# Joint products completed in place in two buffers, two more h blocks stored without their sums, premade sums at a wider pace

## The chip, the cores and the metric

One core of a Trainium2 chip runs the whole kernel in one launch. The metric is the device time of one execution in microseconds. All matrix products run on TensorE (PE in the profile), elementwise work on VectorE (DVE) and ScalarE (ACT); transfers are issued from the queues of SyncE (SP), GpSimd (POOL) and, for the very last store, ScalarE. The profile's times are microseconds from the span's start.

## The reference, cut to what matters

```python
a = einsum("bsd,ed->bse", x, dft_hid_re);  b = einsum("bsd,ed->bse", x, dft_hid_im)
A = einsum("ts,bse->bte", dft_seq_re, a) - einsum("ts,bse->bte", dft_seq_im, b)   # Fourier mixing
gate = einsum("bsd,df->bsf", x, W_gate);   up = einsum("bsd,df->bsf", x, W_up)
B = einsum("bsf,fd->bsd", where(gate > 0, gate, 0) * up, W_down)                  # gated MLP
g = sigmoid((x * gate_w).sum(-1))
return g * A + (1 - g) * B          # S = 2048, D = 512, F = 1792, float32
```

## The kernel before, in words

Every matrix operand is float32. It is split into a high part (a cast on ScalarE) and a low part (a subtraction on VectorE), and each product is three matmuls of 128x128 by 128x512: high by low, low by high, high by high. In the trace the parts carry h and l at the end of their names: xh and xl are the input's, wah, wal, wb0h, wb1l and wd the gate and up weights', lh and ll the down weights', ch and cl the right operands' of the later stages, wh and wl the left operands' of the last stage.

Products are done by schemes of the Strassen kind: seven products of sums of blocks (numbered 1 to 7) in place of eight, and for the sequence transform 26 products, one to a turn. The kernel's stages in order are:

1. **Gate and up**, blocks c = 0 to 6 of F for each half q of the sequence (q is 0 or 1). Blocks 0 and 1 of the first half come first, then c = 2 to 6 with both halves. A block ends with h, the product of the rectified gate and of up. From c = 3 on, class `Joined` computes one of the seven products (product 2 of gate and up) for both halves together by a second scheme over halves and blocks, class `JointW`, with seven short steps of three matmuls; from c = 4 on (`FOURS`) product 4 is treated the same way. I call these the joint steps 1 to 7. Their results leave PSUM by ScalarE copies or VectorE adds and are added to the block's own sums in `done` and `last`. Joint weights are made from the block's weights (buffers jws, jw); jx and kx are the joint right operands, jv and jo the joint intermediate values and results, u the sums of gate and up before the last multiplication.
2. **The hidden transform** (`SpectralBlock`), with blocks 0 and 1 of the second half of gate and up between.
3. **Two down rounds** (`Down`, one for each half of the sequence), whose right operands hr are read back from HBM (tensor hd).
4. **The sequence transform** (`Sequence`), 26 turns of 48 matmuls each, whose operands r and l are read from HBM and summed on the way; results are kept in PSUM or in js buffers and combined at the turns' ends.

h goes to HBM in `h_out`. Normally `h_sums` makes two pairs of sums of it on VectorE (buffers hs, four additions of 512 columns) and stores seven forms in all, which the down round reads. A pair of blocks named in the set `RAW`, as (half, pair), is stored without sums, as four forms; then the down round reads four and makes four sums itself (`made`).

Sums of the sequence matrices that many turns share are made early. `form_stored` makes them by DMA alone: a copy into HBM (tensor td) and then an accumulating transfer onto it, both from POOL's queue, paced by a small token instruction each. `form_rights` and `form_lefts` make others on VectorE (buffers rt, lt): two loads, one sum, one store. `put` is a store from SP's queue, `store` one from POOL's. In `form_stored(values, first, gap)` each of the four parts of a value takes two gaps, counted in matmuls.

The order of the work is not written out. Every step has a key, the number of the matmul beside which it is wanted, and a planner (`Plan`) simulates the engines. VectorE's and ScalarE's steps are sorted by a due time worked out backwards from the matmuls that need them; a step may run up to 40 matmuls ahead of its key. Steps that no matmul waits for get a due time from their key (`REST`), capped near the end of the program. Buffers (a "unit" each) are taken from 51 in all, the one idle longest first, so an instruction that first writes a buffer waits for the last user of its former tenant, a store among them. `LEAD`, `RAMP` and `FORM_LEAD` say how many matmuls ahead of use the sequence stage's operands are loaded, summed and split; `prepared` says the same for gate and up weights.

The lines of the joint step and of its results that the change touches most:

```python
slots = {(5, 1): (5, 1), (6, 1): (6,), (7, 0): (3, 7), (3, 0): (2, 4)}   # after which product which joint steps run
two, one = buf("jv"), buf("jv6", (N,))
self.s = {1: two[:, 0], 5: two[:, 1], 6: one[:]}
self.o = [buf(f"jo{q}") for q in range(2)]
```

Of the kernel before, what the change touches and what calls it, by code (L numbers as in the profile page):

```python
# [15 lines left out]
N = 512  # L16
# [2 lines left out]
NT, KD, KF = S // N, D // P, F // P  # L19
HD = D // 2  # L20
UNITS = 51
FOURS, FOUR_KEY, FOUR_W = 4, -100, 40

# [38 lines left out]
DIRECT, PLACE = (9, 10, 11, 14, 15, 20, 21), (0, 2, 3, 1)  # L64
GROUP = {9: 1, 10: 0, 11: 1, 14: 1, 15: 0, 20: 0, 21: 0}
ROOM = {'r': 6, 'l': 4}
LEAD = {'r': {'load': 56, 'sum': 56, 'sums': 8, 'draws': 30, 'hi': 42, 'lo': 34}, 'l': {'load': 40, 'sum': 46, 'sums': 8, 'draws': 56, 'hi': 55, 'lo': 48}}
RAMP = 50
FORM_LEAD = 43


def walk(side, blocks, room, ready=(), drawn={}):
# [197 lines left out]
class Plan:  # L270
# [47 lines left out]
    def due(self):  # L318

        last, n = {}, self.now  # L320
        for s in reversed(self.steps):
            if s.engine == "tensor" and s.key >= 0:
                n -= s.writes[0].size() / N
            if s.engine == "tensor":
                last[s] = min(last.get(s, 1e9), n * self.MATMUL)
            elif s not in last or s.key > 0:
                last[s] = min(last.get(s, 1e9), min(s.key + self.REST, self.now - 8) * self.MATMUL)
            s.due = last[s] - (s.work + self.LANDING if s.name == "dma_start" else 0)
            for x in s.after:
                last[x] = min(last.get(x, 1e9), s.due - self.WAIT - (x.work if x.name != "dma_start" else 0))  # L330
# [91 lines left out]
def kernel(ctx: ExitStack, tc, xP, xG, wgu, wd, cr, ci, wri, gw, out):  # L422
# [66 lines left out]
    def E():  # L489
        return plan  # L490
# [118 lines left out]
    FORM = {1: 0, 2: 1, 3: 2, 5: 3, 7: 4, 6: 5, 4: 6}  # L609


    RAW = {(0, 1), (1, 2), (0, 0), (0, 3), (0, 2), (1, 3)}

    def h_sums(q, c, h, key):
        f = [buf(f"hs{n}") for n in range(2)]
# [27 lines left out]
    class Block:  # L643


        def __init__(self, q, w, banks=PAIRS):
            self.q, self.w, self.banks = q, w, banks
            self.x = {m: X[q, m] for m in ORDER if (q, m) in X}
            self.g = {r: buf("g" + r, (N,)) for r in ("11", "21")}
            self.s = {m: buf(f"s{m}") for m in (5, 6)}  # L650
            self.u = {r: buf("u" + r) for r in ("12", "22")}
            self.h = [buf(f"h{d}") for d in range(2)]

        def run(self):
# [48 lines left out]


        def added(self, r, a, b, key):
            u, h = self.u[r], self.h[int(r[0]) - 1][:, int(r[1]) - 1]
            op(key, lambda: E().vector.tensor_add(u.all, a.all, b.all))
            op(key + 1, lambda: E().vector.scalar_tensor_tensor(h, u[:, 0], 0.0, u[:, 1], op0=OP.max, op1=OP.mult))

    class Joined(Block):  # L710


        def __init__(self, q, w, four=None):
            super().__init__(q, w)
            self.four = four
            if four and q:
                self.banks = {**PAIRS, "y": PAIRS["t"]}
            self.u["11"] = buf("u11")
            if four:
                self.u["21"] = buf("u21")  # L720
            if not q:
                self.s[1] = buf("s1")

        def run(self, joint=None):
            slots = {(5, 1): (5, 1), (6, 1): (6,), (3, 0): (3, 7), (3, 1): (2, 4)}
            order = [(3, 0), (7, 0), (3, 1), (7, 1), (4, 0), (4, 1)]
            fours = {}
            if self.four:
                slots = {(5, 1): (5, 1), (6, 1): (6,), (7, 0): (3, 7), (3, 0): (2, 4)}
                fours = {(6, 0): (5, 1), (7, 0): (6,), (7, 1): (3, 7), (3, 0): (2, 4)}  # L730
                order = [(7, 0), (7, 1), (3, 0), (3, 1)]
            for m, i in [(m, i) for m in (1, 5, 6) for i in range(2)] + order:
                pe(6, self.product, m, i)
                if m == 6 or m == 7 and not self.four:
                    self.half(m, i, plan.now)
                if i:
                    self.evac(m, plan.now)
                for j, some in ((self.four, fours), (joint, slots)) if joint else ():
                    for y in some.get((m, i), ()):
                        j.step(y)  # L740
                        if j is self.four and y == 4:
                            self.last(plan.now)
                if self.four and not joint and (m, i) == (7, 1):
                    self.last(plan.now)

        def last(self, key):
            u, y, o = self.u["21"], self.banks["y"], self.four.o[self.q]
            op(key + 1, lambda: E().vector.tensor_sub(u.all, y.all, o.all))
            op(key + 2, lambda: E().vector.scalar_tensor_tensor(
                self.h[1][:, 0], u[:, 0], 0.0, u[:, 1], op0=OP.max, op1=OP.mult))  # L750

        def done(self, key, joint):
            self.added("11", self.s[1] if self.q == 0 else self.banks["x"], joint.o[self.q], plan.now)
            super().done(key)

        def one(self, m, i, k, n):
# [61 lines left out]
    class JointW:  # L818


        def __init__(self, w, x, key, m=2):
            self.w, self.x, self.m = w, x, m
            raw, s = buf("jws", [4, P]), w.raw[0][:, 1] if m == 2 else w.raw[1][:, 0]
            self.t = buf("jw", [2, 4, P], F32R)
            two, one = buf("jv"), buf("jv6", (N,))
            self.s = {1: two[:, 0], 5: two[:, 1], 6: one[:]}
            self.o = [buf(f"jo{q}") for q in range(2)]
            self.bank = PAIRS["x" if m == 2 else "t"]
            op(key - 30, lambda: combine(raw[:, 0], s[:, 0, 1], s[:, 1, 1], 1))
            op(key - 30, lambda: combine(raw[:, 2], s[:, 0, 0], s[:, 0, 1], -1))  # L830
            op(key - 29, lambda: combine(raw[:, 1], raw[:, 0], s[:, 0, 0], -1))
            op(key - 28, lambda: combine(raw[:, 3], s[:, 1, 0], raw[:, 1], -1))
            op(key - 24, lambda: E().scalar.copy(self.t[:, 0], raw.all))
            op(key - 20, lambda: E().vector.tensor_sub(self.t[:, 1], raw.all, f32(self.t[:, 0])))
# [16 lines left out]
        def evac(self, y, key):  # L851
            Y, M = (self.bank[n] for n in range(2))
            s, o, e = self.s, self.o, E()
            if y in (1, 5, 6):
                op(key, lambda: e.scalar.copy(s[y], M if y == 5 else Y))
            elif y == 4:
                op(key, lambda: e.scalar.copy(o[0][:, 1], Y))
            else:
                q, i, ps, t = {3: (1, 0, M, 6), 7: (1, 1, Y, 5), 2: (0, 0, M, 1)}[y]
                op(key, lambda: e.vector.tensor_add(o[q][:, i], ps, s[t]))  # L860


    def gate(t, key):
# [271 lines left out]
    def formed(side, blocks, trails, parts, first, last, source, name, shape):  # L1135
# [4 lines left out]
        for part, trail in chains:  # L1140
            old = None
            for x, v in trail:
                b = buf(name, shape)
                op(key - FORM_LEAD, lambda b=b, x=x, part=part: load(b.all, source(part, x)))
                if old:
# [1 line left out]
                    p, q, s = signed(*SUMS[side][v - blocks], SIGNS[side], v)  # L1147
                    p, q = (o, b) if p == a else (b, o)
                    op(key, lambda o=o, p=p, q=q, s=s: combine(o.all, p.all, q.all, s))
                    op(key + 5, lambda o=o, v=v, part=part: put(source(part, v), o.all))  # L1150
                old = x, b
                key += gap

# [396 lines left out]
    for b in start:  # L1550
        b.done(plan.now + 8)

    form_stored([16, 35, 37, 18], 156, 22)
    form_rights([28, 38], 864, 1253)


    spectral = Spectral()

    def prepared(c, ahead=82):
        w = Weights(c)  # L1560
        w_prep(w, plan.now, ahead)
        return w
# [47 lines left out]
    for n in range(2):  # L1610
# [2 lines left out]
            op(key + k + 6 * n, lw.sum, m, n)  # L1613
        for m, k in ((5, -90), (6, 10), (3, 48), (7, 88), (2, 130), (4, 170)):
            lw.split(m, n, key + k + 14 * n, 8)
    form_stored([19], plan.now + 20, 25)
    Down(lw, 0)
    form_lefts([8], plan.now + -129, plan.now + 104)
    Down(lw, 1)
# [56 lines left out]
```

## Time and profile before

| | |
|---|---|
| median of 3 runs | 771.38 us (769.3 to 772.09) |
| the profiled execution's own time | 769.49 us |
| its span | 767.7 us |
| TensorE | 762.1 us busy, 99% |
| VectorE | 677.7 us busy, 88% |
| ScalarE | 407.8 us busy, 53% |
| GpSimd | 95.0 us busy, 12% |
| granted TensorE clock | 1.000 |
| DMA traffic | 197.51 MB, mean 257 GB/s |

TensorE's busy time takes in matmuls that overlap in its pipeline, so a short standstill shows in the starts of neighbouring matmuls sooner than in the share. VectorE and ScalarE run beside TensorE; their idle time costs nothing as long as what they make arrives in time.

### The profile page before, as it was taken

What the parts mean: (1) busy time and instruction counts of PE and PEld (TensorE: products, weight loads), DVE (VectorE), ACT (ScalarE), POOL (GpSimd) and SP (SyncE); (2) the same over time, 40 slices, a digit from 0 to 9 for tenths busy, and PEclk for the clock granted to TensorE, in tenths of its full rate; (3) what the DMA queues carried; (4) which work ended last, traced back from release to release, by engine and by line L of the source; (5) the groups of instructions that cost most, each with busy time, mean ns of one, the idle gap of its engine ahead of it and who ended that gap; (6) DMA issues with size and microseconds to landing.
All of it is one profiled execution on the core that took longest, in us unless ns stands there. A gap on an engine that the chain in (4) does not pass through costs nothing.

```text
span 767.7 us, 9404 instructions
## 1 busy us (share of the span) xinstructions
PE 762.1 (99%) x3357; PEld 627.4 (82%) x3357; DVE 677.7 (88%) x757; ACT 407.8 (53%) x497; POOL 95.0 (12%) x118
## 2 busy tenths in 40 slices
PE   9999999999999999999999999999999999999998
PEld 7788888788788888888888888888888888888886
DVE  6999787867699885999999869998989999979987
ACT  5766454343444452656644536645674556827633
POOL 0111211112000000003510000130210210113010
PEclk9999999999999999999999999999999999999999
DMA  9385887758698999989599798998995998989984
GB/s 320 120 218 125 223 256 203 217 142 222 186 319 302 365 403 365 371 307 323 150 242 369 257 410 310 285 242 168 327 261 174 255 254 278 242 198 281 298 191 109
DMA packets 65503, 197.51 MB, mean 257 GB/s; under 512 B 6960, under 2 KB 7472, under 8 KB 65456
## 3 DMA queue, kind: packets, MB, share of 16 engines
q1 hardware_dynamic: 51776, 147.49, 52.8%
q0 software_dynamic: 13536, 49.29, 32.2%
q8 instruction: 26, 0.43, 0.2%
q14 instruction: 21, 0.17, 0.1%
q10 hardware_dynamic: 144, 0.13, 0.1%
HBM read 149.68 MB, written 68.17 MB: 284 GB/s over the span
## 4 chain that ended last, share of the span: by engine, by line
PE 88%; DVE 7%; DMA 2%; issue 2%; ACT 1%; DVEq 0%; ACTq 0%
PE ps L267 88%; DVE cl L267 2%; DVE u L267 1%; DVE r L267 1%; DMA hd<-h 1%; DMA hd<-hs 1%; DVE wl L267 1%; DVE h L267 1%; DVE js L267 0%; ACT ch L267 0%; DVE jws L267 0%; DVE wb1l L267 0%; DVE jw L267 0%; DVE jo L267 0%; DVE ps L267 0%
## 5 line engine op out<-in xcount | busy, mean ns | idle before, releaser
L267 PE MATMUL ps<-ch,wl 128*128 128x512 f32 (+1 forms) x420 | 162.7, 387 | 0.1
L267 PE MATMUL ps<-cl,wh 128*128 128x512 f32 (+1 forms) x420 | 162.7, 387 | 0.0
L267 PE MATMUL ps<-ch,wh 128*128 128x512 f32 (+1 forms) x420 | 162.5, 387 | 0.0
L267 ACT CAST ch<-r 128x1024 fp32r<-128x1024 f32 x104 | 105.3, 1052 | 95.2 <-DVE r L267 83.0
L267 DVE TENSOR_TENSOR cl<-r,ch 128x1024 fp32r<-128x1024 f32 x104 | 124.3, 1221 | 3.8 <-ACT ch L267 3.2
L267 PEld LDWEIGHTS ps<-ch,wl 128*128 128x128 f32 x420 | 78.9, 188 | 16.6 <-DVE js L267 0.5
L267 PEld LDWEIGHTS ps<-cl,wh 128*128 128x128 f32 x420 | 78.9, 188 | 16.6 <-DVE cl L267 0.4
L267 PEld LDWEIGHTS ps<-ch,wh 128*128 128x128 f32 x420 | 78.9, 188 | 15.9
L267 PE MATMUL ps<-ch,ll 128*128 128x512 f32 x196 | 76.2, 389 | 0.0
L267 PE MATMUL ps<-cl,lh 128*128 128x512 f32 x196 | 76.2, 389 | 0.0
L267 PE MATMUL ps<-ch,lh 128*128 128x512 f32 x196 | 76.2, 389 | 0.0
L267 ACT CAST ch<-hr 128x1024 fp32r<-128x1024 f32 (+1 forms) x56 | 51.0, 944 | 36.7 <-DVE hr L267 22.7
L267 ACT COPY s<-ps 128x1024 f32<-128x1024 f32 (+1 forms) x48 | 41.7, 874 | 50.1 <-PE ps L267 38.8
L267 DVE TENSOR_TENSOR cl<-hr,ch 128x1024 fp32r<-128x1024 f32 (+1 forms) x56 | 59.4, 1087 | 6.8 <-ACT ch L267 5.4
L267 POOL COPY tk<-tk 128x1 f32<-128x1 f32 x20 | 23.0, 1152 | 250.3 <-ACT tk L267 250.3
L267 ACT CAST wh<-l 128x1024 fp32r<-128x1024 f32 x38 | 39.5, 1053 | 16.3 <-DVE l L267 13.0
L267 DVE TENSOR_TENSOR wl<-l,wh 128x1024 fp32r<-128x1024 f32 x38 | 46.0, 1220 | 0.3 <-ACT wh L267 0.2
L267 PE MATMUL ps<-xh,wb0l 128*128 128x512 f32 x112 | 43.8, 391 | 0.0
L267 PE MATMUL ps<-vh,xl 128*128 128x512 f32 x112 | 43.7, 390 | 0.0
L267 PE MATMUL ps<-xl,wb0h 128*128 128x512 f32 x112 | 43.6, 389 | 0.0
L267 PE MATMUL ps<-xh,wb1l 128*128 128x512 f32 x112 | 43.6, 389 | 0.0
L267 PE MATMUL ps<-vh,xh 128*128 128x512 f32 x112 | 43.6, 389 | 0.0
(161 smaller groups left out, 1502.9 us busy)
## 6 DMA issues: line engine op xcount, KB each, us to landing
l<-ad SPq DMA_DIRECT2D x32, 512.0 KB, 7.5
hr<-hd SPq DMA_DIRECT2D x30, 512.0 KB, 6.0
r<-td SPq DMA_DIRECT2D x24, 512.0 KB, 7.4
td<-cr POOLq DMA_DIRECT2D x20, 512.0 KB, 5.2
td<-ci POOLq DMA_DIRECT2D x20, 512.0 KB, 6.0
wr<-wgu SPq DMA_DIRECT2D x16, 512.0 KB, 7.5
ad<-a SPq DMA_DIRECT2D x16, 512.0 KB, 7.4
r<-cr SPq DMA_DIRECT2D x16, 512.0 KB, 6.8
```

The source lines that it names most:

```text
L267: getattr(getattr(nc, self.engine), self.name)(*map(ap, self.a), **{k: ap(x) for k, x in self.k.items()})
```

## The change

- `RAW` gains the pair (1, 1): blocks 2 and 3 of the second half are stored without sums.
- `JointW` keeps its three intermediate values and four results in two buffers (ja, jb) instead of four (jv, jv6, two jo); each result is completed in the place of its intermediate value. `done` and `last` go through a new function `summed`, which adds the block's own sums onto the joint results in two additions of 512 columns each, and then multiplies. `added` sums into the block's s buffer. The u buffers go.
- With both joint products, joint steps 2 and 4 of product 2 run after (7, 1) instead of after (3, 0).
- `FOUR_KEY` -100 to -90, `FOUR_W` 40 to 35; weights of gate and up are loaded 66 instead of 82 matmuls ahead.
- `form_stored` first makes the values 16, 35, 19, 18 with a gap of 25 (was 16, 35, 37, 18 with 22); 37 takes the later place that 19 had. `form_rights` makes 38 in the old stretch and 28 in a later one. Formed values are stored from POOL's queue.
- `LEAD`, `RAMP`, `FORM_LEAD` and the cap of the due times change.

```diff
-FOURS, FOUR_KEY, FOUR_W = 4, -100, 40
+FOURS, FOUR_KEY, FOUR_W = 4, -90, 35
...
-LEAD = {'r': {'load': 56, 'sum': 56, 'sums': 8, 'draws': 30, 'hi': 42, 'lo': 34}, 'l': {'load': 40, 'sum': 46, 'sums': 8, 'draws': 56, 'hi': 55, 'lo': 48}}
-RAMP = 50
-FORM_LEAD = 43
+LEAD = {'r': {'load': 56, 'sum': 56, 'sums': 4, 'draws': 36, 'hi': 42, 'lo': 36}, 'l': {'load': 44, 'sum': 46, 'sums': 8, 'draws': 56, 'hi': 55, 'lo': 48}}
+RAMP = 40
+FORM_LEAD = 44
...
-                last[s] = min(last.get(s, 1e9), min(s.key + self.REST, self.now - 8) * self.MATMUL)
+                last[s] = min(last.get(s, 1e9), min(s.key + self.REST, self.now + 40) * self.MATMUL)
...
-    RAW = {(0, 1), (1, 2), (0, 0), (0, 3), (0, 2), (1, 3)}
+    RAW = {(0, 1), (1, 2), (0, 0), (1, 1), (0, 3), (0, 2), (1, 3)}
...
         def added(self, r, a, b, key):
-            u, h = self.u[r], self.h[int(r[0]) - 1][:, int(r[1]) - 1]
-            op(key, lambda: E().vector.tensor_add(u.all, a.all, b.all))
-            op(key + 1, lambda: E().vector.scalar_tensor_tensor(h, u[:, 0], 0.0, u[:, 1], op0=OP.max, op1=OP.mult))
+            h = self.h[int(r[0]) - 1][:, int(r[1]) - 1]
+            op(key, lambda: E().vector.tensor_add(b.all, a.all, b.all))
+            op(key + 1, lambda: E().vector.scalar_tensor_tensor(h, b[:, 0], 0.0, b[:, 1], op0=OP.max, op1=OP.mult))
...
-                slots = {(5, 1): (5, 1), (6, 1): (6,), (7, 0): (3, 7), (3, 0): (2, 4)}
+                slots = {(5, 1): (5, 1), (6, 1): (6,), (7, 0): (3, 7), (7, 1): (2, 4)}
...
         def last(self, key):
-            u, y, o = self.u["21"], self.banks["y"], self.four.o[self.q]
-            op(key + 1, lambda: E().vector.tensor_sub(u.all, y.all, o.all))
-            op(key + 2, lambda: E().vector.scalar_tensor_tensor(
-                self.h[1][:, 0], u[:, 0], 0.0, u[:, 1], op0=OP.max, op1=OP.mult))
+            self.summed(self.banks["y"], self.four, self.h[1][:, 0], E().vector.tensor_sub, key)
+
+        def summed(self, bank, joint, h, f, key):
+            a, b = (joint.o[self.q, i] for i in range(2))
+            for i, o in enumerate((a, b)):
+                op(key + 1, lambda i=i, o=o: f(o, bank[:, i] if isinstance(bank, Buf) else bank[i], o))
+            op(key + 2, lambda: E().vector.scalar_tensor_tensor(h, a, 0.0, b, op0=OP.max, op1=OP.mult))
 
         def done(self, key, joint):
-            self.added("11", self.s[1] if self.q == 0 else self.banks["x"], joint.o[self.q], plan.now)
+            self.summed(self.banks["x"] if self.q else self.s[1], joint, self.h[0][:, 0], E().vector.tensor_add, plan.now - 1)
...
-            two, one = buf("jv"), buf("jv6", (N,))
-            self.s = {1: two[:, 0], 5: two[:, 1], 6: one[:]}
-            self.o = [buf(f"jo{q}") for q in range(2)]
+            a, b = buf("ja"), buf("jb")
+            self.o = {(0, 0): a[:, 0], (1, 1): a[:, 1], (1, 0): b[:, 0], (0, 1): b[:, 1]}
+            self.s = {1: a[:, 0], 5: a[:, 1], 6: b[:, 0]}
...
-                q, i, ps, t = {3: (1, 0, M, 6), 7: (1, 1, Y, 5), 2: (0, 0, M, 1)}[y]
-                op(key, lambda: e.vector.tensor_add(o[q][:, i], ps, s[t]))
+                ps, t = {3: (M, 6), 7: (Y, 5), 2: (M, 1)}[y]
+                op(key, lambda: e.vector.tensor_add(s[t], ps, s[t]))
...
-                    op(key + 5, lambda o=o, v=v, part=part: put(source(part, v), o.all))
+                    op(key + 5, lambda o=o, v=v, part=part: store(source(part, v), o.all))
...
-    form_stored([16, 35, 37, 18], 156, 22)
-    form_rights([28, 38], 864, 1253)
+    form_stored([16, 35, 19, 18], 156, 25)
+    form_rights([38], 864, 1253)
+    form_rights([28], 1231, 1655)
...
-    def prepared(c, ahead=82):
+    def prepared(c, ahead=66):
...
-    form_stored([19], plan.now + 20, 25)
+    form_stored([37], plan.now + 79, 25)
```

## Rows read from the trace of the kernel before

**Rows 1.** The page, part 1: busy us (share of the span) xinstructions.
```profile
PE 762.1 (99%) x3357; PEld 627.4 (82%) x3357; DVE 677.7 (88%) x757; ACT 407.8 (53%) x497; POOL 95.0 (12%) x118
```

**Rows 2.** Windows: stretch and its length, busy us (xinstructions), clock, DMA share, GB/s.
```profile
120.00:220.00 100.00, 98.72 (x432) 80.46 (x431) 74.39 (x108) 40.87 (x66) 10.88 (x20) 1.00 0.74 205
...
240.00:320.00 80.00, 80.00 (x354) 66.20 (x354) 64.85 (x99) 35.68 (x44) 0.00 (x0) 1.00 1.02 379
320.00:400.00 80.00, 80.00 (x355) 66.24 (x354) 77.84 (x86) 48.88 (x58) 20.52 (x12) 1.00 0.83 255
...
440.00:480.00 40.00, 40.00 (x178) 33.14 (x177) 32.28 (x30) 18.49 (x20) 1.75 (x2) 1.00 0.94 358
```

**Rows 3.** Timeline of TensorE at four gaps: start, length, operation, xcount [idle before].
```profile
133.56 0.84 PE L267 MATMUL ps<-jx,jw 128*128 128x512 f32 x3
135.19 0.96 PE L267 MATMUL ps<-jx,jw 128*128 128x512 f32 x3 [0.79 <-ACT jv L267]
135.99 0.40 PE L267 MATMUL ps<-xh,wb1l 128*128 128x512 f32 x1
...
143.96 0.39 PE L267 MATMUL ps<-xh,wb1h 128*128 128x512 f32 x1
144.40 0.50 PE L267 MATMUL ps<-xh,wal 128*128 128x512 f32 x1
...
203.15 0.39 PE L267 MATMUL ps<-xh,wb0h 128*128 128x512 f32 x1
203.90 0.74 PE L267 MATMUL ps<-kx,jw 128*128 128x512 f32 x2 [0.36 <-DVE jw L267]
...
644.67 0.39 PE L267 MATMUL ps<-ch,wh 128*128 128x512 f32 x1
645.14 0.50 PE L267 MATMUL ps<-ch,wl 128*128 128x512 f32 x1
```

**Rows 4.** Groups by line and form, VectorE: busy us, mean ns | idle before.
```profile
L267 DVE TENSOR_TENSOR hr<-hr,hr 128x1024 f32<-128x1024 f32 x16 | 19.5, 1221 | 0.0
...
L267 DVE TENSOR_TENSOR u<-ps,jo 128x1024 f32<-128x1024 f32 x10 | 12.1, 1218 | 0.2
...
L267 DVE TENSOR_TENSOR hs<-hs,h 128x512 f32<-128x512 f32 x8 | 5.5, 689 | 0.1
```

**Rows 5.** Timelines of VectorE and TensorE in the two down rounds.
```profile
364.58 1.22 DVE L267 TENSOR_TENSOR cl<-hr,ch 128x1024 fp32r<-128x1024 f32 x1
...
369.05 0.39 PE L267 MATMUL ps<-cl,lh 128*128 128x512 f32 x1
...
475.15 1.21 DVE L267 TENSOR_TENSOR l<-l 128x1024 f32<-128x1024 f32 x1
476.28 0.68 DVE L267 TENSOR_TENSOR cl<-hr,ch 128x512 fp32r<-128x512 f32 x1
476.88 1.22 DVE L267 TENSOR_TENSOR cl<-r,ch 128x1024 fp32r<-128x1024 f32 x1
...
479.21 0.39 PE L267 MATMUL ps<-cl,lh 128*128 128x512 f32 x1
```

**Rows 6.** Timelines of VectorE and ScalarE in gate and up, with waits.
```profile
110.58 0.69 DVE L267 TENSOR_TENSOR ws<-wr 128x512 f32<-128x512 f32 x1 [1.42 <-DMA wr<-wgu]
...
134.56 0.59 ACT L267 COPY jv<-ps 128x512 f32<-128x512 f32 x1 [2.84 <-DMA hd<-hs]
135.79 1.29 DVE L267 TENSOR_TENSOR jo<-ps,jv 128x512 f32<-128x512 f32 x2 [6.44 <-DMA hd<-hs]
143.76 0.59 ACT L267 COPY jo<-ps 128x512 f32<-128x512 f32 x1 [1.36 <-DVE u L267]
190.15 1.23 DVE L267 TENSOR_TENSOR wal<-wr,wah 128x1024 fp32r<-128x1024 f32 x1 [2.00 <-DMA hd<-h]
203.16 0.68 DVE L267 TENSOR_TENSOR jw<-jws,jw 128x512 fp32r<-128x512 f32 x1
```

**Rows 7.** Everything that touches the h sums hs: time of their stores to landing.
```profile
DMA to landing us min/median/max: 5.4/7.8/10.8
```

More of the change, by code (lines that the diff above doesn't have):

```diff
@@ L650, in __init__ @@
             self.s = {m: buf(f"s{m}") for m in (5, 6)}
-            self.u = {r: buf("u" + r) for r in ("12", "22")}
             self.h = [buf(f"h{d}") for d in range(2)]
@@ L717, in __init__ @@
                 self.banks = {**PAIRS, "y": PAIRS["t"]}
-            self.u["11"] = buf("u11")
-            if four:
-                self.u["21"] = buf("u21")
             if not q:
@@ L856, in evac @@
             elif y == 4:
-                op(key, lambda: e.scalar.copy(o[0][:, 1], Y))
+                op(key, lambda: e.scalar.copy(o[0, 1], Y))
             else:
-                q, i, ps, t = {3: (1, 0, M, 6), 7: (1, 1, Y, 5), 2: (0, 0, M, 1)}[y]
-                op(key, lambda: e.vector.tensor_add(o[q][:, i], ps, s[t]))
+                ps, t = {3: (M, 6), 7: (Y, 5), 2: (M, 1)}[y]
+                op(key, lambda: e.vector.tensor_add(s[t], ps, s[t]))
     def gate(t, key):
```

## The prediction

> **What bounds the kernel now.** I read the page's first two parts, then TensorE's waits, then its timeline for gaps, then the table of windows, and last who was late at each gap. The page shows TensorE busy 99% of the span at the full granted clock, VectorE 88%, ScalarE 53% [rows 1]. The number of matmuls isn't changed, so only the time in which TensorE stands can be saved. Its steady step is read from a window without a gap: 80 us hold 355 matmuls, two of them cut by the edges, so 80 / 353 = 0.227 us each in 320 to 400 [rows 2]. Against this step the timeline shows five places where TensorE stood, and each is followed by one step of 0.34 instead of 0.227, which I count to it:
> - from 133.56 three joint matmuls, the next at 135.19 instead of 134.24, then 0.11 lost in restarting: 1.06 us [rows 3];
> - 143.96 to 144.40, where the next block's first product waits for a joint result to leave its bank: 0.33. The same pattern stands once more, at 181.03 to 181.48: 0.34 [rows 3];
> - 203.15 to 203.90: 0.64, on the split weight of the joint product [rows 3];
> - 644.67 to 645.14, in the sequence stage: 0.35 [rows 3].
>
> Together 2.37 us in the stage of gate and up and 0.35 later. The rest of what isn't matmul (start, the last store) is touched by one edit only. So this execution of 769.49 us (767.7 span, 1.8 around it) can't fall below about 769.49 - 2.37 - 0.35 = 766.8 by these edits. The median of the runs shown, 771.38, lies 1.9 above this execution, the lowest run 769.3 beside it.
>
> **Part by part.** *Stored without sums, blocks 2 and 3 of the second half.* It takes away two blocks' h sums: 16 such sums stand in the trace for four blocks (the row shows eight; two groups of four have the same length), so 8 x 0.60 us start to start [rows 4, 5] = 4.8 us of VectorE at about 85 to 130 us, and four stores of 512 KB for two of 256 KB. It matters for the gap at 133.56: TensorE there waited for the ScalarE copy that frees the bank, at 134.56, which had waited 2.84 us for the store of a sum, hd<-hs, because its buffer had held that sum; VectorE's jo stood 6.44 us behind the same store [rows 6]. These are the sums of block 3, second half, which this edit removes. I take the full 1.06 us. Bounds: 1.06 gained, or nothing if the buffer falls to another tenant that is also being stored (hd<-h, as at 190.15 [rows 6]); I take the gain, because the joint results also need two buffers instead of four and the blocks' u buffers go, so fewer buffers change hands. In the second down round it adds four sums of 1024, in place of three loads of 512 KB: 4 x 1.13 = 4.5 us of VectorE [rows 4, 5]. That stretch has 32.28 us busy of 40 at 440 to 480 [rows 2]; nothing on TensorE, 2.3 us without that cover (last rival).
>
> *Joint step (2,4) twelve matmuls earlier.* In blocks 4 to 6 the joint results left the bank with six matmuls (1.36 us) to the next block's start; the copy at 143.76 had waited 1.36 us for VectorE and ran 0.59 [rows 6]. Now twelve more matmuls, 2.7 us, lie between. That covers a lateness of 0.33 and 0.34: 0.67 gained. Ahead of it, the bank's other half is reused 15 matmuls after product 7 instead of 27; that still is 3.4 us for an add of 0.69, and I charge nothing; up to 0.3 a block if VectorE has 3 us queued.
>
> *Joint weights of the second joint product five matmuls earlier, weight loads 16 later.* The late split ran at 203.16 behind a VectorE that had lost 2.0 us at 190.15 waiting for an h store [rows 6]. Five matmuls are 1.13 us, more than the 0.64. But weights now are loaded 3.6 us later, and at 110.58 VectorE already waited 1.42 for them [rows 6]: such a wait could grow to 5.0. VectorE is 74% busy in 120 to 220 [rows 2], so most is caught up. I take 0.64 gained; from 0.64 to a loss of 1.0 at each of two or three blocks.
>
> *Completed in place.* 14 adds of 1024 become 28 of 512 (ten in one row, four more have the other joint input) [rows 4]. A 512 add costs 0.60 start to start, a 1024 one 1.13 [rows 5], so 14 x 0.07 = 1.0 us of VectorE over 130 us, hidden beside the matmuls. An in-place add isn't dearer: hr<-hr,hr is one, 1.22 us, like u<-ps,jo [rows 4]. [...]
>
> *Premade sums.* A sum every 50 matmuls rather than 44 thins the accumulating transfers; value 28's four sums (4.5 us of VectorE [rows 4, 5]) go from about 200 to 288 us to 283 to 380; stores of formed values go from SP's queue to POOL's, behind accumulates there. The values are read long after; SP no longer stands for them. I charge nothing. Without cover it is the last rival's: in 320 to 400 VectorE has 77.84 of 80 us busy [rows 2].
>
> *Leads and due times of the sequence stage.* No instruction is added; the order on VectorE, ScalarE and the queues shifts by 2 to 10 matmuls. One of 26 turns shows a wait, 0.35. Bounds: 0.35 gained; 0.35 at five turns, 1.8 lost. I take zero. The later due times at the end let the last operand splits go ahead of outputs: between 1 us gained and 1 lost, I take zero.
>
> The sum is 1.06 + 0.67 + 0.64 = 2.37 us: 769.49 - 2.37 = 767.1 for an execution like the profiled one. Added to the median's distance of 1.9 it gives 769.0. Some of this distance should go too: the store that held up 133.56 is of a kind that lands after 5.4 to 10.8 us, 7.8 in the median [rows 7], so another run can wait up to some 3 us longer there, and that wait goes whole. I therefore put the median between 767.1 and 769.0, nearer to the upper end because some new small waits are likely: 768.6 us, 0.36% below 771.38.
>
> **Rivals.**
> *The waits come back elsewhere* (22%): every buffer gets another owner and the order is planned anew, so stores of h hold up other instructions, as at 190.15, and later weights take back what the joint step gives. For it: two of the four gaps come from who held a buffer. Against: fewer buffers, less to store. Time: between 769.49 and the old median plus 1, 770.9.
>
> *More than the sum* (10%): the distance of 1.9 came all from landings in the joint stage, and the wait at 644.67 goes too: 771.38 - 1.9 - 2.37 - 0.35 = 766.8.
>
> *VectorE runs out in the down rounds* (13%). TensorE's operands there lead by little: the split ending at 365.80 is used at 369.05, lead 3.25; the one ending at 476.96 at 479.21, lead 2.25 [rows 5]. Should all 4.5 us of value 28's sums fall between VectorE's last idle time and 369, TensorE waits 1.3; should the four new sums fall ahead of 479, 2.3; the sequence stage then starts behind and loses 0.35 at each of ten turns. Together 7.1, 769.49 - 2.37 + 7.1 = 774.2. It outweighs the gain from 2.4 us of new waits on. Against: 15 us idle on VectorE in 240 to 320, where 4.5 us become free [rows 2], and operands at the sequence's start are asked for ten matmuls later.
>
> **Numbers.** The forecast has 55%, its own range 767.0 to 770.2. The range for all is 766.6 to 772.8: about one in ten below, in the second rival, and one in ten above, in the third. 0.5% is 3.9 us, what a measurement here can tell from no change: faster means under 767.5, slower over 775.2. Faster: the second rival and a fifth of the forecast, 20%. Slower: the third's upper half, 6%. No change: 74%.
>
> **What would show it.** Right: no gap over 0.2 us in TensorE's timeline from 120 to 220 us, four hd<-hs stores instead of eight, no VectorE wait for a store of a sum, the copy after product 4 ending over 2 us ahead of the next block. Wrong: a wait for wr<-wgu over 3 us on VectorE before a gap (weights), a gap at the end of either down round or at several turns (VectorE), or a clean joint stage with the median still at 771 (the distance wasn't there).

## The result, and the profile after

The changed kernel takes 772.51 us (median of 20 runs, 771.31 to 773.78). The kernel before, measured beside it, takes 769.61 (20 runs, 768.30 to 773.08). The ratio on record is 1.0028, 95% interval 1.0019 to 1.0038: 0.28% slower, inside the predicted range, but the forecast was a gain, 0.36% below the median shown. (Here and below the ratio is the one on record, with its interval; it is not the quotient of the two medians, which would be 1.0038 here.) The profiled executions lie 1.8 us apart as well: 771.31 against 769.49, spans 769.5 and 767.7.

The page's first part of the changed kernel, to be read beside [rows 1]:

```profile
PE 761.6 (99%) x3357; PEld 626.5 (81%) x3357; DVE 676.9 (88%) x767; ACT 407.2 (53%) x497; POOL 107.1 (14%) x128
```

Only GpSimd moved, 95.0 to 107.1 us. The windows of [rows 2], of the changed kernel (stretch and length; busy us of PE, PEld, DVE, ACT, POOL; clock, DMA share, GB/s):

```profile
120.00:220.00 100.00, 99.74 (x438) 81.72 (x437) 75.19 (x119) 42.62 (x69) 12.88 (x25) 1.00 0.73 204
240.00:320.00 80.00, 80.00 (x354) 66.27 (x353) 62.62 (x97) 37.90 (x47) 2.15 (x4) 1.00 0.99 373
320.00:400.00 80.00, 78.60 (x344) 64.12 (x343) 72.42 (x79) 43.26 (x55) 21.58 (x13) 1.00 0.83 271
440.00:480.00 40.00, 40.00 (x178) 33.12 (x177) 35.73 (x35) 17.62 (x19) 0.90 (x1) 1.00 0.97 362
```

Two things stand in them. From 120 to 220 us there are six matmuls more than before: the gate and up stage did gain. From 320 to 400 us, where TensorE had no gap, it now has 344 matmuls instead of 355, and VectorE, though it has value 28's sums to make there, shows 72.42 us instead of 77.84: it waited.

TensorE's loss by stage is its start-to-start times, each less the steady 0.2267 us, summed over the stage:

| us lost by TensorE | start, 0 to 40 | gate and up, 100 to 240 | first down round, 360 to 420 | sequence, 500 to 760 |
|---|---|---|---|---|
| before | 1.54 | 2.67 | 0.00 | 0.63 |
| after | 0.91 | 1.22 | 4.06 | 0.62 |
| difference | -0.63 | -1.45 | +4.06 | -0.01 |

Together +1.97, of which the span shows 1.8. Of the 4.06, 3.9 are four standstills. TensorE's timeline around them (start, length, operation, form, xcount, idle before and what ended it):

```profile
366.70 0.39 PE L267 MATMUL ps<-ch,ll 128*128 128x512 f32 x1
367.27 0.50 PE L267 MATMUL ps<-cl,lh 128*128 128x512 f32 x1 [0.18 <-DVE cl L267]
...
391.65 0.39 PE L267 MATMUL ps<-ch,ll 128*128 128x512 f32 x1
392.27 0.50 PE L267 MATMUL ps<-cl,lh 128*128 128x512 f32 x1 [0.23 <-DVE cl L267]
...
396.30 0.39 PE L267 MATMUL ps<-ch,ll 128*128 128x512 f32 x1
397.68 0.50 PE L267 MATMUL ps<-cl,lh 128*128 128x512 f32 x1 [0.99 <-DVE cl L267]
...
409.82 0.39 PE L267 MATMUL ps<-ch,ll 128*128 128x512 f32 x1
411.63 0.50 PE L267 MATMUL ps<-cl,lh 128*128 128x512 f32 x1 [1.42 <-DVE cl L267]
```

Each waits for a low part cl from VectorE. With the restart of 0.11 behind each (a first step of 0.33 to 0.35 us) they are 0.45, 0.51, 1.26 and 1.69 us. VectorE's timeline ahead of the last three:

```profile
372.62 2.35 DVE L267 TENSOR_TENSOR cl<-hr,ch 128x1024 fp32r<-128x1024 f32 x2
...
376.03 1.21 DVE L267 SCALAR_TENSOR_TENSOR rt<-rt 128x1024 f32<-128x1024 f32 x1
...
383.18 2.42 DVE L267 TENSOR_TENSOR cl<-hr,ch 128x1024 fp32r<-128x1024 f32 x2
...
391.53 1.83 DVE L267 TENSOR_TENSOR cl<-hr,ch 128x512 fp32r<-128x512 f32 x2 [4.19 <-ACT ch L267]
...
404.69 1.21 DVE L267 TENSOR_TENSOR z<-ps,s 128x1024 f32<-128x1024 f32 x1
```

VectorE stood 4.19 us for ScalarE's ch. It came back at 391.53 with no lead left, and the operands of the next 20 us came late one after another. ScalarE in turn waited for a transfer:

```profile
389.93 1.57 ACT L267 CAST ch<-hr 128x1024 fp32r<-128x1024 f32 x2 [5.58 <-DMA td<-rt]
```

ScalarE wrote into the buffer that had held a premade sum, rt, and could not until its store had landed. That sum was made at 376.03. GpSimd's timeline says why the store was so late:

```profile
369.74 14.70 POOL L267 COPY tk<-tk 128x1 f32<-128x1 f32 x1 [4.25 <-ACT tk L267]
384.38 0.53 POOL L267 DMA_DIRECT2D td<-cr  x1
384.89 0.56 POOL L267 DMA_DIRECT2D td<-rt  x1
...
399.16 5.65 POOL L267 COPY tk<-tk 128x1 f32<-128x1 f32 x1
404.75 0.53 POOL L267 DMA_DIRECT2D td<-ci  x1
```

The token that paces the accumulating transfers, a copy of one column, took 14.70 us, and the store stood behind it in GpSimd's queue. It was issued at 384.89, 7.7 us after the sum was ready. Through these 14.70 us VectorE ran 15 instructions end to end, counting the one already under way, all with both inputs in SBUF; the copy ended at 384.44, when VectorE had begun the second of two cl some 0.07 us later than usual (the pair at 383.18 takes 2.42 us, an unbroken one 2.35, at 372.62). Whether that pause let the copy in or the copy made the pause, the trace doesn't tell. The second long copy ended at 404.81, just after VectorE began an addition with an operand in PSUM (z at 404.69). The kernel before had such a copy too, at nearly the same place:

```profile
370.62 10.13 POOL L267 COPY tk<-tk 128x1 f32<-128x1 f32 x1 [4.62 <-ACT tk L267]
```

That the copy is held because it reads SBUF while VectorE reads both its inputs there is the author's estimate from these rows; e4 and e8 below try a token that only writes.

In gate and up the forecast came true in part. The stores of h sums are four instead of eight, and all lie far behind the joint products (tile hs of the changed kernel: count, issue time min/median/max in ns, first and last start):

```profile
L267 SPq DMA_DIRECT2D hd<-hs x4: 359/364/371, 309.6 to 358.4; - x4
```

The gaps of [rows 3] at 133.56, 143.96 and 203.15 are gone, and 181.03 with them. A new one of 0.53 us stands at 126.12. Ahead of it VectorE waited for weights, which are loaded later now, and ScalarE's copy waited for VectorE; that the first makes the second is only argued here, and e5 below tests it (VectorE and ScalarE):

```profile
115.01 0.69 DVE L267 TENSOR_TENSOR ws<-wr 128x512 f32<-128x512 f32 x1 [1.23 <-DMA wr<-wgu]
...
125.70 1.01 ACT L267 COPY s<-ps 128x1024 f32<-128x1024 f32 x1 [1.31 <-DVE h L267]
```

### The profile page after: what moved, and what is told of

It reads as the page before. It is cut to its first block, busy times and chain, and to the rows that moved or that the text cites. A ratio compares the mean times of both kernels' runs of the same rounds, so it can differ in the third digit from the quotient of the medians.

```text
span 769.5 us, 9391 instructions
## 1 busy us (share of the span) xinstructions
PE 761.6 (99%) x3357; PEld 626.5 (81%) x3357; DVE 676.9 (88%) x767; ACT 407.2 (53%) x497; POOL 107.1 (14%) x128
## 5 line engine op out<-in xcount | busy, mean ns | idle before, releaser
L267 POOL COPY tk<-tk 128x1 f32<-128x1 f32 x20 | 28.8, 1442 | 132.8 <-ACT tk L267 102.8
L267 PEld LDWEIGHTS ps<-cl,lh 128*128 128x128 f32 x196 | 36.8, 188 | 12.0 <-DVE cl L267 4.4
L267 PE MATMUL ps<-xh,wb0h 128*128 128x512 f32 x112 | 43.6, 389 | 0.0
```

What stands on the lines that cost most here:

```text
L267: getattr(getattr(nc, self.engine), self.name)(*map(ap, self.a), **{k: ap(x) for k, x in self.k.items()})
```

## The experiments

Two theories for the first down round. **Q**: the loss needs three things together, value 28's sums made in that round, their stores in GpSimd's queue, and the copy that holds this queue. The rival: VectorE has too much to do there, as the third rival of the prediction had it, and value 28's sums are what is too much. The ratios below are to the kernel before, with 95% intervals. What TensorE lost by stage in the profiled run (worked out as above) and the median times; the sequence column ends in every kernel with the same matmul, the last of 512 columns, since the shorter ones behind it would count as gain (by this count the kernel before has 0.65 and the changed one 0.61):

| kernel | gate and up | 240 to 360 | first down round | sequence | us | ratio |
|---|---|---|---|---|---|---|
| e1_sp_store | 1.20 | 0.00 | 1.70 | 0.60 | 768.60 | 0.9984 (0.9972 to 0.9995) |
| e2_rights_early | 1.10 | 1.08 | 0.00 | 1.10 | 769.02 | 0.9993 (0.9980 to 1.0007) |
| e3_before_late_rights_pool | 3.90 | 0.03 | 0.00 | 0.95 | 771.26 | 1.0018 (1.0005 to 1.0031) |
| e4_token_memset | 0.78 | 0.00 | 0.47 | 0.64 | 768.15 | 0.9982 (0.9970 to 0.9994) |
| e5_memset_weights82 | 2.72 | 0.00 | 0.48 | 0.60 | 768.75 | 0.9994 (0.9980 to 1.0008) |
| e6_memset_rights_mid | 1.33 | 0.03 | 0.78 | 0.77 | 768.51 | 0.9984 (0.9975 to 0.9993) |
| e7_joint_only | 1.60 | 0.70 | 0.00 | 0.86 | 769.46 | 1.0003 (0.9994 to 1.0012) |
| e8_before_memset | 3.17 | 0.02 | 0.00 | 0.63 | 769.62 | 1.0004 (0.9994 to 1.0014) |
| e9_raw_only | 3.03 | 0.01 | 0.00 | 1.17 | 770.08 | 0.9997 (0.9987 to 1.0007) |
| e10_slot_only | 3.47 | 0.03 | 0.00 | 0.62 | 770.58 | 1.0010 (0.9998 to 1.0023) |
| e11_weights_only | 11.94 | 0.15 | 0.00 | 0.62 | 777.11 | 1.0080 (1.0057 to 1.0103) |

**e1_sp_store**, the changed kernel with the stores of formed values back in SP's queue:

```diff
-                    op(key + 5, lambda o=o, v=v, part=part: store(source(part, v), o.all))
+                    op(key + 5, lambda o=o, v=v, part=part: put(source(part, v), o.all))
```

> The changed kernel with one word back: formed values are stored from SP's queue again. Theory Q (queue): in the first down round the store of value 28's third sum waits on POOL behind a token copy that takes 14.7 us, ScalarE's split needs that sum's buffer, and VectorE and TensorE stand behind it. Then the gaps at 391 to 410 us (3.46 us in the changed kernel's trace) go, the gap of 0.45 at 367 may stay, and the time falls by 3 us, from 772.5 to 769.5, the level of the kernel before. Rival D (demand): it is the 4.5 us of VectorE work that value 28's later sums bring to 283 to 380 us. Then the gaps stay and the time stays at 772 to 773.

GpSimd's timeline of e1:

```profile
371.29 14.70 POOL L267 COPY tk<-tk 128x1 f32<-128x1 f32 x1 [4.98 <-ACT tk L267]
385.92 0.54 POOL L267 DMA_DIRECT2D td<-cr  x1
```

The copy is held for the same 14.70 us, and the three standstills from 391 on are gone: only accumulating transfers stand behind it now, and nobody waits for them soon. Two gaps remain ahead of them, at 362.96 and 367.42, 1.6 us together; the second is a larger form of the changed kernel's first, and why it is larger isn't settled.

**e2_rights_early**, the changed kernel with value 28 made in the old stretch, the store left in GpSimd's queue:

```diff
-    form_rights([38], 864, 1253)
-    form_rights([28], 1231, 1655)
+    form_rights([28, 38], 864, 1253)
```

> The changed kernel with value 28's sums back beside 38's at 200 to 288 us, still stored from POOL. Theory Q: no formed value of this kind is in POOL's queue when the slow token copies come, so the gaps of the first down round go: 769 us. Rival D: VectorE has 4.5 us less there, the gaps go too, the one at 367 as well: 768.5 us. Rival R (the rest: blocks without sums, leads, weights loaded later): the gaps stay, 772 us. With e1 this tells Q and D from R.

All four standstills of the down round are gone, although a copy there is still held 10.13 us. About 1.1 us come up between 240 and 360 us, where the sums now are. Moving either the store or the sums away is enough: both conditions of Q are needed. e2 alone doesn't speak against the rival, since it takes VectorE's work away as well; e1 and e4 do.

**e4_token_memset**, the changed kernel in which the token on GpSimd writes its column instead of copying one. It writes the column that ScalarE has written, so it waits for ScalarE as before. Nothing else differs but the name by which the planner finds the token, and in the traces the order of instructions on TensorE, VectorE, ScalarE and SyncE is the same as in the changed kernel.

```diff
-        op(key, lambda: plan.gpsimd.tensor_copy(tk[:, 2, n:n + 1], tk[:, 1, n:n + 1]))
+        op(key, lambda: plan.gpsimd.memset(tk[:, 1, n:n + 1], 0.0))
```

> The changed kernel with one difference: the token instruction on POOL is a memset that writes one column instead of a copy that reads one; the order on the other four queues is the same. Theory Q with its cause: the copy is held while VectorE works on two operands from SBUF without a break (its row takes 14.7 us at 369.74, where VectorE never stands), and an instruction that reads nothing isn't held. Then the memset rows take under 1 us, value 28's third store is issued near 377 instead of 384.9, and the gaps at 391 to 410 go: 769.5 us. If the token is held whatever it does (rival P: POOL is slow to start any instruction there), the row stays over 5 us and the time at 772.5. Rival D: the token rows may shorten, but the gaps stay: 772.5.

The row of the twenty tokens of e4 (duration min/median/max in ns), and GpSimd's timeline:

```profile
L267 POOL MEMSET tk<- x20: 98/98/100, 31.0 to 389.6; 128x1 f32 x20
```

```profile
369.67 0.10 POOL L267 MEMSET tk<- 128x1 f32 x1 [4.66 <-ACT tk L267]
369.91 0.53 POOL L267 DMA_DIRECT2D td<-cr  x1
377.47 0.55 POOL L267 DMA_DIRECT2D td<-rt  x1 [7.02 <-DVE rt L267]
```

No token is held; the store goes out at 377.47, as soon as its sum is ready, instead of at 384.89. The same sums on VectorE, the same store in GpSimd's queue, and the three standstills are gone: the rival falls. The time is 768.15, by the medians 4.36 below the changed kernel (3.5 by the two ratios to the kernel before), and 0.18% below the kernel before. It is the fastest version that was run, with e1 and e6 inside its interval. The token that only writes took 0.098 us in the median and 0.100 at most over 20 tokens, where the copies of the changed kernel took up to 14.70.

**e8_before_memset**, the same edit on the kernel before:

> The kernel before with the memset token. In its trace the token copy is held for 10.1 and 4.8 us in the first down round, but only premade-sum transfers of a value used far later stand behind it on POOL. Theory Q: holding the token costs nothing where no store that frees a buffer is queued behind it, so the time stays within 0.8 us of 769.6 while the memset rows are all 0.1 us. [...]

Ratio 1.0004: no gain, though the tokens fall from up to 10.13 us to 0.099 in the median and 0.385 at most. In the kernel before only premade transfers stood behind the held copy. The held token is old; the change put something behind it that others wait for.

**e3_before_late_rights_pool**, the kernel before with the later value 28 and the stores in GpSimd's queue and no other edit (the diffs of e1 and e2, the other way round):

> The kernel before with only two parts of the change: value 28's sums later, and formed values stored from POOL. Theory Q: the store falls behind a token copy (10 us long there, in the trace of before) and TensorE gets a gap of 2 to 4 us in the first down round: slower than before by 2 to 4 us. Rival D: as the lead there goes down to 3.2 us in the kernel before, 4.5 us more of VectorE work cost about 1.3 us: 771. Rival R: no change, within 1 us.

This missed: the down round has no gap. GpSimd's timeline of e3:

```profile
353.16 2.63 POOL L267 COPY tk<-tk 128x1 f32<-128x1 f32 x1
...
375.36 0.86 POOL L267 COPY tk<-tk 128x1 f32<-128x1 f32 x1
376.17 0.53 POOL L267 DMA_DIRECT2D td<-ci  x1
379.89 0.55 POOL L267 DMA_DIRECT2D td<-rt  x1 [3.19 <-DVE rt L267]
```

The tokens come at other times and the one just ahead of the store takes 0.86 us; the longest hold is 2.63 us. The old pace of 22 alone doesn't explain that, for the kernel before has it too and its token was held for 10.13 us. So the third condition of Q is, by the author's estimate, a matter of phase, of where a token falls beside VectorE's runs; neither that nor what sets the phase was tested by itself.

Its 0.18% stands in gate and up, 3.90 us instead of 2.67, and its cause stays open. Of the difference of 1.23 us, 1.0 lies ahead of 203 us, where VectorE, ScalarE and SyncE run the same instructions in the same order as in the kernel before (1.43 us instead of 1.06 after 133.57, and a new gap of 0.62 at 197.60). e8, which has the order of before throughout, has 1.23 us at 131.03 in place of 1.06 at 133.56. So one profile of this stage is no finer than about 1 us, which bears on every gate and up figure in the table.

**e6_memset_rights_mid**, e4 with value 28 in between, to see whether its sums make the gap at 367:

```diff
-    form_rights([28], 1231, 1655)
+    form_rights([28], 1100, 1400)
```

> The changed kernel with the memset token, and value 28's sums at matmuls 1100 to 1400 (about 254 to 322 us, where VectorE has idle time) instead of 1231 to 1655. It keeps a gap of 0.45 us at 367, in the first down round. Theory D in small: the last of value 28's sums take VectorE's lead there. Then the gap goes and the time falls by about 0.4, unless the sums make a new gap in the hidden transform, as in the kernel with all sums early (0.66 at 244, 0.36 at 286). Rival: the gap comes from the waits at 337 to 341 us; then it stays.

No sum of value 28 begins after 326.1 us, and the gap is still there, 0.74 us at 366.91. So it doesn't need these sums inside the round. In e2, where the last of these sums is done by 297 us, it is gone, so they may still bear on it from further ahead. What makes VectorE late at 367 isn't settled; it is 0.45 us of the changed kernel.

**e5_memset_weights82**, e4 with the gate and up weights loaded as early as before:

```diff
-    def prepared(c, ahead=66):
+    def prepared(c, ahead=82):
```

> The changed kernel with the memset token, and gate and up weights loaded 82 matmuls ahead again instead of 66. The memset-token kernel keeps gaps in gate and up at 126 us (0.29 to 0.53 us in three traces), 118 and 151 to 202 (0.1 each). Theory W: these come from weights that land later (VectorE waits 1.2 us for them at 115 and ScalarE's copies queue behind). Then the gap at 126 goes and the time falls by 0.3 to 0.7 us from 768.15. Rival: they come from the two-half additions and the order of ScalarE's copies; then they stay and the time stays within 0.3 of 768.15.

The gap at 126 goes, as theory W has it, but one of 2.22 us comes at 118.22 (ScalarE's timeline of e5, then VectorE's):

```profile
117.66 0.62 ACT L267 CAST jw<-jws 128x512 fp32r<-128x512 f32 x1 [2.51 <-DVE ws L267]
118.18 1.04 ACT L267 CAST wb1h<-ws 128x1024 fp32r<-128x1024 f32 x1
119.92 0.58 ACT L267 ACTIVATE ps<-ps 128x512 f32<-128x512 f32 x1 [0.70 <-DVE s L267]
```

```profile
117.53 2.35 DVE L267 TENSOR_TENSOR s<-ps,s 128x1024 f32<-128x1024 f32 x2
```

The copy out of the bank that TensorE waits for (119.92) stands behind two weight casts, and when they are done it waits another 0.70 us for VectorE's second addition s, which came last. In place of the expected gain of 0.3 to 0.7 us the stage lost 2.72 instead of 0.78. Whether the time is worse than e4's isn't shown: the intervals overlap.

Then the parts of gate and up alone, each on the kernel before. Theory **J**: the prediction's terms of 1.06, 0.67 and 0.64 hold one by one. Rival **W**: waits come back elsewhere.

**e7_joint_only**, in-place results, the earlier joint step and the new keys of the second joint product's operands and weights, no other edit:

> The kernel before with the joint part of the change alone: results completed in place in two buffers, no u buffers, step (2,4) earlier, second joint product's operands and weights with the new leads; h sums, premade sums, weight loads and the sequence stage as before. Theory: of the 2.37 us that TensorE stood in gate and up, 0.67 (two blocks' starts) and 0.64 (the late split) go, 1.06 (the copy behind the store of an h sum) goes only if the buffer has another former tenant: 767.2 to 768.3 us against 769.6. Rival: the stalls move to other buffers and copies, as in the changed kernel, where 1.0 of 2.37 came back; then 768.5 to 769.

Ratio 1.0003. The four gaps of before are gone, and one of 1.03 us stands at 117.93. ScalarE of e7 there, and VectorE:

```profile
118.44 0.58 ACT L267 ACTIVATE ps<-ps 128x512 f32<-128x512 f32 x1 [2.86 <-DVE s L267]
```

```profile
116.06 2.35 DVE L267 TENSOR_TENSOR s<-ps,s 128x1024 f32<-128x1024 f32 x2
```

ScalarE's copy that frees the bank comes after VectorE's two in-place additions here, as in e5. That isn't in the nature of adding in place: in the changed kernel the copy goes between the two, and the second addition waits for it, without a gap (VectorE of the changed kernel):

```profile
118.04 1.23 DVE L267 TENSOR_TENSOR s<-ps,s 128x1024 f32<-128x1024 f32 x1 [0.47 <-ACT ps L267]
```

Another 0.7 us comes between 240 and 360 us, most of it at 244.89.

**e9_raw_only**: the pair (1, 1) added to `RAW`, nothing else.

> The kernel before with one edit: blocks 2 and 3 of the second half are stored without their h sums. The prediction's term was 1.06 us (the standstill after 133.56, a ScalarE copy that waits for the store of an h sum). Theory J (the term is right and independent): that gap is gone, four hd<-hs stores instead of eight, the sum of gaps in 100 to 240 us falls by 0.9 to 1.2, and 768.4 to 768.8 against 769.6 for before (ratio 0.998 to 0.999). Rival W (waits come back, since every buffer gets another owner when the order is planned anew): the gap at 133.56 goes, but new ones of 0.3 to 1.3 us in sum come up in 100 to 240 us or in the second down round with its four more sums, and 769.3 to 770.0 (0.9995 to 1.0005).

W: the gap at 133.56 is gone, and 1.27 us at 112.96 and 0.73 at 152.72 are there instead. TensorE and ScalarE of e9 at the first:

```profile
112.96 0.39 PE L267 MATMUL ps<-xh,wb1h 128*128 128x512 f32 x1
114.35 0.50 PE L267 MATMUL ps<-xh,wb1l 128*128 128x512 f32 x1 [1.00 <-ACT s L267]
```

```profile
112.77 1.05 ACT L267 CAST wb0h<-ws 128x1024 fp32r<-128x1024 f32 x1 [2.46 <-DVE ws L267]
113.72 0.58 ACT L267 COPY s<-ps 128x512 f32<-128x512 f32 x1
```

The weight came late, its cast went ahead of the copy that frees the bank. (By the time alone theory J is not quite excluded: the interval 0.9987 to 1.0007 touches its upper end.)

The gap at 203.15 is gone as well, though nothing at the joint weights was changed. VectorE's split and TensorE's next joint matmuls in e9:

```profile
203.18 0.68 DVE L267 TENSOR_TENSOR jw<-jws,jw 128x512 fp32r<-128x512 f32 x1
```

```profile
204.40 0.84 PE L267 MATMUL ps<-kx,jw 128*128 128x512 f32 x3
```

The split runs when it did before (203.16, [rows 6]). But TensorE had stood longer by then and begins the matmul ahead of these at 204.17 instead of 203.15, so it finds the operand ready. The gap behind a late VectorE went here when TensorE had lost 1.02 us ahead of it; by the author's estimate it would grow when such time is saved: such gaps are not terms of a sum.

**e10_slot_only**: `(7, 1): (2, 4)` in place of `(3, 0): (2, 4)`, nothing else.

> The kernel before with one edit: joint steps 2 and 4 of product 2 twelve matmuls earlier, after (7, 1). The prediction's term was 0.67 us (the standstills after 143.96 and 181.03). Theory J: both are gone and nothing else grows: 768.8 to 769.1 against 769.6 (0.9988 to 0.9994). Rival W: ScalarE's copies and VectorE's adds of joint results, now asked for earlier, push another step out, as the joint part alone did at 117.93 with 1.03 us: 769.4 to 770.3 (0.9998 to 1.0008), with a new gap of 0.3 us or more in 110 to 240 us.

W: 143.96 and 181.03 are gone, and 1.05 us at 165.91 and 0.40 at 173.09 are new. The gap behind the store of an h sum grew from 1.06 to 1.27 us, and the one at 203.15 is gone here too. TensorE of e10:

```profile
167.09 0.96 PE L267 MATMUL ps<-kx,jw 128*128 128x512 f32 x3 [0.78 <-DVE jw L267]
```

**e11_weights_only**:

```diff
-FOURS, FOUR_KEY, FOUR_W = 4, -100, 40
+FOURS, FOUR_KEY, FOUR_W = 4, -90, 35
...
-    def prepared(c, ahead=82):
+    def prepared(c, ahead=66):
```

> The kernel before with the weights' edits alone: joint weights of product 4 asked for ten matmuls later by key and split in 35 matmuls instead of 40, gate and up weights loaded 66 instead of 82 matmuls ahead. The prediction's term was 0.64 us gained at 203.15, bounded by a loss of 1.0 us at each of two or three blocks. Theory J: the gap at 203.15 is gone, no gap on a weight, 768.8 to 769.1 (0.9988 to 0.9994). Rival W: VectorE waits over 2 us for wr<-wgu before a gap near 117 to 126, 152 to 165 or 190 to 202; 769.8 to 771.5 (1.0003 to 1.0025).

In the code it is `FOUR_KEY` that moves the second joint product's right operands, ten matmuls later, and `FOUR_W` that asks for its weights five matmuls earlier, as the prediction has it.

W, and far beyond its price: 0.8% slower, with one standstill of 5.26 us after 117.69. (The profiled run, 778.12, is the slowest of six that go down to 772.53, so the standstill is not that long in each.) VectorE and SP's queue of e11:

```profile
118.68 0.69 DVE L267 TENSOR_TENSOR ws<-wr 128x512 f32<-128x512 f32 x1 [4.92 <-DMA wr<-wgu]
```

```profile
105.23 4.62 SPq L267 DMA_DIRECT2D hd<-h  x3
109.89 1.12 SPq L267 DMA_DIRECT2D wr<-wgu  x1
```

The weight load stands behind three stores of h in SP's queue and goes out at 109.89. In the changed kernel the same three take 1.85 us and the load goes out at 106.83; that the other edits make the weights' edit bearable there is what this suggests; it wasn't tested by itself. The gap that the edit was meant to remove is still there. The same matmul stands for the same split, 0.69 us where the kernel before has 0.64 (TensorE of e11, 8.7 us behind the kernel before by then):

```profile
212.62 0.73 PE L267 MATMUL ps<-kx,jw 128*128 128x512 f32 x2 [0.42 <-DVE jw L267]
```

The 5.26 us did not come alone (windows of e11, clock in the third column from the end):

```profile
117.50:123.20 5.70, 0.60 (x4) 0.18 (x2) 4.49 (x6) 3.07 (x5) 0.81 (x1) 0.85 0.48 89
123.20:128.20 5.00, 5.00 (x12) 3.94 (x13) 4.96 (x10) 1.13 (x3) 0.96 (x3) 0.50 0.47 144
128.20:133.00 4.80, 4.80 (x23) 3.92 (x21) 4.80 (x8) 1.79 (x3) 0.51 (x1) 0.98 0.78 139
```

## Why the prediction was wrong, step by step

**The step that failed** is the one under premade sums: "stores of formed values go from SP's queue to POOL's, behind accumulates there. The values are read long after; SP no longer stands for them. I charge nothing." It asked who reads the stored value, and not who takes over the buffer that it is stored from. That buffer was ScalarE's next ch. It also looked at the transfers in GpSimd's queue and not at the tokens between them, of which one was held 10.13 us in the trace of before already. The price in the profiled run is 3.5 of the first down round's 4.06 us: the last three gaps, which e1, e2 and e4 each take away by another of the three conditions. The sum gave 767.1 us for an execution like the profiled one, and 771.31 was measured. Of these 4.2 us, the held store is 3.5, the gap at 367 0.45 and the three terms below 0.9; the start gave 0.6 back.

**The 1.06 us** of h blocks stored without sums: the wait for the store of a sum went, as predicted. Alone (e9) the edit brings nothing that can be told from zero: ratio 0.9997, other gaps take the place.

**The 0.67 us** of the earlier joint step: both gaps went in e10 and in the changed kernel. The changed kernel's first copy of these steps ended at 139.93, 3.3 us ahead of the next block's 143.22. That is over 2 us, as forecast. Alone again no gain, 1.0010.

**The 0.64 us** of the joint weights: the gap at 203.15 went in the changed kernel, but barely: the split ended at 201.95 and TensorE's next matmul began at 202.01. The five matmuls are not what removes it: with the weights' edits alone (e11) it stays, 0.69 us, and in e9 and e10 it goes without them. The wait for later weights, "could grow to 5.0", was well judged, 4.92 in e11; the bound on what of it reaches TensorE, "a loss of 1.0 at each of two or three blocks", was too small there: 5.26 in one place. In the changed kernel the new gap is 0.53, if it is the weights'.

The three terms were added as if the gaps were independent. Made together with the joint part they gave 1.45 of 2.37 in the profiled pair (five kernels with all of it lose 0.78 to 1.33 us in gate and up, three without lose 2.67 to 3.90); made one by one, nothing that can be told from zero, or a loss. The first rival, the waits that come back elsewhere, had e7, e9, e10 and e11 right. It was near the truth for the down round too, where an instruction waited for the store of its buffer's former tenant; but it named stores of h, and its time of 770.9 was 1.6 too low.

**The median's distance.** The forecast of 768.6 used 1.9 us between the profiled run and a median of three. Over 20 runs the kernel before has 769.61, and the profiled run's own time is 769.49. There was no distance to lose; 771.38 was a small sample. Without it the forecast would have been 767.1, further from what was measured. That the measured time fell into the range is luck: nothing that the range was made of has the held store in it.

**Completed in place, four more sums in the second down round, leads**: nothing in the changed kernel's trace speaks against zero. The second round has 35.73 us of VectorE in 40 at 440 to 480 and no gap; the sequence stage lost 0.62 us instead of 0.63. In e9 the four sums alone make no gap in the down rounds either; the leads were not tried by themselves.

**The third rival** named the right place and an operand that comes late there, and the wrong reason: VectorE was not short of time, it stood for 4.19 us, and with the same work on it the three gaps are gone in e4.

Left open: the gap at 367 (0.45 us), and the 0.63 us at the start, a figure that runs from 0.85 to 1.54 over kernels in which VectorE and SyncE start in the same order. The changed kernel's median lies 1.2 us above its profiled run, which was its fastest; where its slower runs lose more wasn't profiled. The clock is not the cause: all 20 runs have a granted clock of 0.999 or 1.000.

## What to carry to other kernels

Before a store is moved to another queue, list what is issued ahead of it there, small synchronizing instructions too, and who next writes the buffer that it empties; the reader of the stored data is the lesser question. Where VectorE runs without a break on operands in SBUF, a token on GpSimd should write and not read (0.1 us in e4 instead of up to 14.7 in the changed kernel). Gaps of an engine that waits for others are no sum of terms: made one at a time, two edits that removed their gaps brought nothing, and a third left its gap standing. When a step is priced at the gap that it removes, ask what the next late engine does when TensorE arrives earlier.

## What the hardware showed that was not expected

- A GpSimd copy of one column was held for 14.70 us (10.13 in the kernel before) while VectorE ran instructions with operands in SBUF end to end, not for one of them but for 15 in a row. It came through beside a pause of some 0.07 us, and a second one, held 5.65 us, beside an addition from PSUM. Memsets of the same column took 0.098 to 0.100 us, all 20 of them (e4), and 0.385 at most in e8.
- After TensorE had stood 5.26 us in e11, the granted clock was 0.50 in the window of 5.00 us behind it, which holds 12 matmuls, about 0.42 us each instead of 0.227: by an estimate from that count 2.3 us on top of the standstill. Behind the gap of 2.22 us in e5 the first step was 0.34 us; behind the changed kernel's gaps of 0.45 to 1.69 us it was 0.33 to 0.35, and the steps after it 0.22 to 0.24.
